# Queries of the first eight blocks through VectorE, and a later start for the second group's weights

## The chip, the cores and the metric

The kernel runs on one core of one Trainium2 chip. The metric is the device time of one launch in microseconds (us). Engines are named as the profile names them: PE is TensorE (matmuls), PEld its weight loads, DVE VectorE, ACT ScalarE, POOL GpSimd, and SP SyncE, the queue that issues nearly all DMAs, in program order.

## The reference

Two stages, one after the other, all in float32:

```python
# q, k, v: (8 batches, 8 heads, 576 tokens, 64)
scores = scale * q @ k.T
Dmat   = where(i >= j, gamma[h] ** (i - j), 0)     # a decay per head
x      = (scores * Dmat) @ v                       # -> (4608 tokens, 512)
h      = x @ w_in                                  # w_in (512, 2048)
out    = (h * erf(softplus(h))) @ w_out            # w_out (2048, 512)
```

The weights come as float64 and are rounded to float32 in the kernel.

## The kernel before

**Attention.** The 4608 tokens are cut into 36 blocks of 128 (`pieces`): of each batch's 576 tokens four blocks, and the last 64 tokens of two batches share one. So blocks 8, 17, 26 and 35 are two-piece blocks. The work on a block is three functions: `transposes(i)` makes qT and kT (64 of the head dimension x 2 heads on the partitions), `scores(i)` multiplies them on PE and lets DVE apply the decay mask (tile sT), `outputs(i)` multiplies sT by v, adds the running state of the batch, and lets DVE scale the result into x. The list `stages` puts `transposes(i + 1)` ahead of `outputs(i)` and `scores(i + 1)` behind it (L68 to L73); `attend(n)` works that list off. Four PSUM tiles with the tag "at" serve all three.

**Two ways to a transpose.** From block SQUARES = 8 on, q and k are loaded as squares (`load_squares`, L122): 32 partitions per DMA, four DMAs per one-piece block and name, 112 KB each, with a contiguous run of 896 bytes per row and head; a DVE transpose of 32 x 32 squares (L314) then gives qT or kT. For a two-piece block it is eight DMAs of 48 KB with runs of 384 bytes. In blocks 0 to 7 they come as rows (`load_rows`, L135): two DMAs of 128 KB per block and name, runs of 256 bytes, then four PE transposes into PSUM (L320) and an ACT copy (L322 for q, L326 for k). k of one-piece blocks and v are always loaded as rows too, for the outputs. The square tiles have two buffers per name (q's rows use the same two buffers), k's and v's row tiles four. `transposes(i)` ends by issuing the q load (and the k squares, if any) of block i + 2, `outputs(i)` that of k and v of block i + 3.

**Two big products.** Nine chunks of 512 tokens, and four groups of the 2048 hidden columns: 36 pairs (g, c), group by group. Each pair has a `First` (x times w_in, then softplus, erf, multiply) and a `Second` (times w_out, added to the running output). Both use seven products in place of eight for a 2 x 2 block product (Strassen-Winograd), so operands are sums of quarters, made by DVE (`tt`, L99). One product is 8 matmuls of 256 columns: L478 in `First`, L585 in `Second`. The first chunk of the first group uses the plain product (L532).

**Order of the work.** A string in the main part (L708) interleaves the first chunk by hand: `a` is one attention stage, `p` a part of the plain product, `w` loads one part of weights, a digit so many rounding steps. Then the loop L735 runs over `First(n + 1)` and `Second(n)` in turn, and `run(steps, rounds)` puts one attention stage and a given number of rounding steps behind every product. Nine chunks of group 0 carry all the attention, so it ends about a third of the way in (the last squares are turned at 318 us).

**Weights.** A group has eight parts of 512 KB (four of w_in, two DMAs each; four of w_out, one DMA each). `load_weights()` issues the next part into a ring of four buffers (`wraw`, L224). `rounding()` (L232) is a generator that rounds one part in five steps: an ACT pair (L246, L247), three DVE steps (L251, L255, L259), and a last step with DVE (L264) and POOL or DVE (L266, L267), which for groups 1 to 3 also issues the next part. The last part of w_in and of w_out is followed by four steps of sums (L99). The first eight parts are issued by the string; the loop issues two more at the head of the second and two at the head of the third block `First` (n = 1 and 2).

Of the kernel before, what the change touches and what calls it, by code (L numbers as in the profile page):

```python
# [11 lines left out]
FP32 = mybir.dt.float32  # L12
# [6 lines left out]
P = 128  # L19
B, H, S, D = 8, 8, 576, 64  # L20
D_MODEL, D_FF = 512, 2048
NP = H // 2
# [32 lines left out]
def kernel(  # L55
# [10 lines left out]
    nc = tc.nc  # L66
# [65 lines left out]
                )  # L132
        return t

    def load_rows(i, name, src, bufs):  # L135
        if name == "q":
            t = raw.tile([P, NP, P * D // SQ], FP32, tag="qs", name="raw_q", bufs=bufs)
            t = t.rearrange("p a x -> p (a x)")[:, : H * D].rearrange("p (h d) -> p h d", h=H)
        else:
            t = raw.tile([P, H, D], FP32, tag=name, name=f"raw_{name}", bufs=bufs)  # L140
        for b, s0, n, r0 in pieces[i]:
            for e in range(2):
                heads = src[b, e * NP : (e + 1) * NP, s0 : s0 + n, :]
                nc.sync.dma_start(out=t[r0 : r0 + n, e::2, :], in_=heads.rearrange("h p d -> p h d"))  # L144
        return t

    def load(i, names="qkv"):
        if i < len(pieces):
            t = loaded.setdefault(i, {})
            for name in names:  # L150
                src = {"q": q, "k": k, "v": v}[name]
                if name == "q" and i < SQUARES:
                    t["q"] = load_rows(i, "q", q, 2)
                elif name == "q":
                    t["qs"] = load_squares(i, "q", q)
                    t["ks"] = load_squares(i, "k", k)
                elif name == "v" or len(pieces[i]) == 1:
                    t[name] = load_rows(i, name, src, 4)

    load(0)  # L160
    cst = cpool.tile([P, CONST_COLS], FP32, name="cst")
# [13 lines left out]
    A11, S3, A12, A22, S1, S2, S4 = range(7)  # L175
    B11, T3, B21, B22, T1, T2, T4 = range(7)
    weights = {}

    def operands(name, g):
        if (name, g) not in weights:  # L180
# [51 lines left out]
    def rounding():  # L232


        while True:
            while not words or words[0][2] > most_g[0]:
                yield
            t, name, g, slot, j, sums = words.pop(0)
            w = operands(name, g)
            dst = w[:, slot : slot + 2, j, :]  # L240
            pairs = t[:, :].rearrange("p (h f two) -> p h f two", h=2, two=2)
            pairs_f = t[:, :].bitcast(FP32).rearrange("p (h f two) -> p h f two", h=2, two=2)
            low, high = pairs[:, :, :, 0], pairs[:, :, :, 1]
            r_f, high_f = pairs_f[:, :, :, 0], pairs_f[:, :, :, 1]
            a_f, a = dst, dst.bitcast(UINT32)
            nc.scalar.activation(a_f, high_f, AF.Abs)  # L246
            nc.scalar.mul(out=r_f, in_=low, mul=2.0**-52)  # L247
            yield


            nc.vector.tensor_scalar(  # L251
                out=a_f, in0=a_f, scalar1=HIGH_LEAST, scalar2=HIGH_MOST, op0=ALU.max, op1=ALU.min
            )
            yield
            nc.vector.tensor_scalar(  # L255
                out=a, in0=a, scalar1=3, scalar2=0x3FFFFFFF, op0=ALU.logical_shift_left, op1=ALU.bitwise_and
            )
            yield
            nc.vector.scalar_tensor_tensor(  # L259
                out=a, in0=high, scalar=0xC0000000, in1=a, op0=ALU.bitwise_and, op1=ALU.bitwise_or  # L260
            )
            yield

            nc.vector.tensor_scalar(out=high, in0=a, scalar1=0xFF800000, scalar2=None, op0=ALU.bitwise_and)  # L264
            engine = nc.vector if (name, g) == ("wa", 0) else nc.gpsimd
            engine.tensor_tensor(out=r_f, in0=high_f, in1=r_f, op=ALU.mult)  # L266
            engine.tensor_tensor(out=a_f, in0=a_f, in1=r_f, op=ALU.add)  # L267
            if g > 0:
                load_weights()
            yield  # L270
            if sums:
                yield from sums(*(w[:, i] for i in range(7)))

    round_step = rounding()

    def round_weights(n=1):
        for _ in range(n):
            next(round_step, None)
# [24 lines left out]
    def transposes(i):  # L303
        t = live[i] = loaded.pop(i)
        if i < SQUARES:
            weigh_values(i)
        for name in "qk":
            tT = t[name + "T"] = att.tile([P, NP, P], FP32, tag=name + "T", name=name + "T")
            if i >= SQUARES:
                for _, _, n, r0 in pieces[i]:  # L310
                    a = r0 // SQ * D
                    squares = t[name + "s"][:, :, a : a + n // SQ * D].rearrange("p h (a d) -> p h a d", d=D)
                    order = "p h (a r) -> p h a r" if name == "q" else "p h (r a) -> p h a r"
                    nc.vector.transpose(  # L314
                        out=tT[:, :, r0 : r0 + n].rearrange(order, r=SQ), in_=squares[:, :, :, :SQ]
                    )
            else:
                pt = ps_at.tile([P, NP, P], FP32, tag="at", name=f"pt_{name}")
                for p in range(NP):
                    nc.tensor.transpose(pt[:, p, :], flat(t[name][:, 2 * p : 2 * p + 2, :]), ident)  # L320
                if name == "q":
                    nc.scalar.copy(  # L322
                        out=tT.rearrange("p h (a r) -> p h a r", r=SQ), in_=pt.rearrange("p h (r a) -> p h a r", r=SQ)
                    )
                else:
                    nc.scalar.copy(out=tT, in_=pt)  # L326
        load(i + 2, "q")

    def scores(i):
# [139 lines left out]
    class First:  # L469
# [3 lines left out]
            self.g, self.c = g, c  # L473

        def product(self, a, acc, start):
            for j in range(GP):
                for d in range(2):
                    nc.tensor.matmul(  # L478
                        acc[:, j * TH : (j + 1) * TH],
                        lhsT=weights["wa", self.g][:, a, d, j * P : (j + 1) * P],  # L480
                        rhs=x[self.g, self.c][a][:, d, :],
                        start=(start and j == 0 and d == 0),
                        stop=(d == 1),
                        skip_group_check=True,
                    )
# [83 lines left out]
    class Second:  # L569
# [9 lines left out]
                nc.sync.dma_start(out=self.o, in_=od[self.c])  # L579

        def product(self, b, acc, start):
            left = self.of.left[b]
            for j in range(GP):
                for tp in range(2):
                    nc.tensor.matmul(  # L585
                        acc[:, tp, :],
                        lhsT=left[:, j * TH + tp * P : j * TH + (tp + 1) * P],
                        rhs=weights["wb", self.g][:, b, j, :],
                        start=(start and j == 0 and tp == 0),
                        stop=(j == GP - 1),  # L590
                        skip_group_check=True,
                    )
# [142 lines left out]
    for b, nxt in zip(blocks[1:], blocks[2:] + [None]):  # L735
        n = order.index((b.g, b.c))
        if isinstance(b, First):
            most_g[0] = order[n - 1][0] + 1
            if n in (1, 2):
                load_weights()  # L740
                load_weights()
            run(b.middle(), (1, 1))
            firsts[n - 1].sums()
            run(seconds[n - 1].first(), (1, 1) if n > 1 else ())
            run(b.last(), (1,) if 1 < n < n_ch else ())
            most[0] = before_chunk(n + 3)
        elif n + 2 < n_s:
            f = firsts[n + 1]
            for step, _ in enumerate(b.middle()):
                attend(min(done[0] + 1, most[0]))  # L750
                if step == 0:
                    f.erf()
                elif step == 1 and n + 2 >= n_ch:
                    operands_x(*order[n + 2])
            if n + 2 < n_ch:
                attend(after_chunk(n + 2))
                operands_x(*order[n + 2])
            run(nxt.first(), (1,))
            f.multiply()
            seconds[n + 1].begin()  # L760
            if n_ch <= n + 3 < n_s:
                load_x(*order[n + 3])
            run(b.last(), (0, 1))
        elif n + 1 < n_s:
            firsts[n + 1].erf()
            seconds[n + 1].begin()
            rest = b.rest()
            for _ in range(3):
                next(rest)
            firsts[n + 1].multiply()  # L770
            run(rest)
            firsts[n + 1].sums((0,))
            first = nxt.first()
            next(first)
            firsts[n + 1].sums((1,))
            run(first)
        else:
            run(b.rest())
# [30 lines left out]
```

## Time and profile before

| | us |
|---|---|
| median of 8 runs | 1039.12 |
| lowest, highest | 1037.62, 1040.63 |
| the profiled execution | 1038.71 |
| its span, first to last instruction | 1036.9 |
| busy: PE, PEld | 1017.8, 874.8 |
| busy: DVE, ACT, POOL | 675.9, 387.6, 125.1 |
| moved by DMA | 167.27 MB, mean 161 GB/s |

The profile's first part gives busy time per engine; PE's is an upper figure, since matmuls overlap and their ends are modelled. The second part cuts the span into 40 slices of some 26 us and writes the busy share of each in tenths. The fourth follows the chain of work that ended last back to the start. The other views are asked of the trace: busy time in chosen stretches, the instructions in order of time (start, length, engine, line, operation, tile written and tiles read, count, and in brackets the idle time before it and what ended it), groups of instructions with count, busy time and mean length, and who waited for whom.

### The profile page before, as it was taken

To read this page: it belongs to the slowest core of one execution; us is meant where nothing else is said; L and a number is where in the kernel's file an instruction comes from. 1 tells how busy PE (TensorE), PEld (TensorE's weight loads), DVE (VectorE), ACT (ScalarE), POOL (GpSimd) and SP (SyncE) were. 2 spreads that over 40 slices of the span, in tenths; PEclk is the share of its full clock that TensorE was granted. 3 is DMA by queue.
4 is the path that set the end of the run, shared out by engine and by line. 5 is a ranking of instruction groups with operands and counts; after the bars stand their busy time and mean duration, and the time that the engine had idled before them with its cause. 6 is when DMAs were issued, how large, how long until landed. Compare 5 with 4: busy or idle time off the path is not lost.

```text
span 1036.9 us, 15904 instructions
## 1 busy us (share of the span) xinstructions
PE 1017.8 (98%) x6322; PEld 874.8 (84%) x6322; DVE 675.9 (65%) x1063; ACT 387.6 (37%) x477; POOL 125.1 (12%) x122
## 2 busy tenths in 40 slices
PE   9899999999999999999999999999999999999998
PEld 8777877778788888888888888888888888888887
DVE  3998867778877645567665656666666655555555
ACT  2353233232342444433443334434443333333332
POOL 2161222321312100100001000100100000000000
PEclk9999999999999999999999999999999999999999
DMA  9989989979984531633274424353333334444433
GB/s 196 214 209 222 253 172 251 217 183 247 230 196 143 176 129 40 233 153 142 61 264 143 164 101 142 143 212 150 125 122 122 122 121 130 131 131 132 127 88 116
DMA packets 148778, 167.27 MB, mean 161 GB/s; under 512 B 97632, under 2 KB 123360, under 8 KB 140640
## 3 DMA queue, kind: packets, MB, share of 16 engines
q1 hardware_dynamic: 147696, 165.47, 56.2%
q8 instruction: 50, 0.82, 0.4%
q10 hardware_dynamic: 1008, 0.79, 0.3%
q14 instruction: 24, 0.20, 0.1%
HBM read 119.02 MB, written 47.19 MB: 160 GB/s over the span
## 4 chain that ended last, share of the span: by engine, by line
PE 79%; DMA 9%; DVE 5%; SPq 5%; issue 1%; ACT 1%; POOL 1%; DVEq 0%; POOLq 0%; ACTq 0%
PE a L585 21%; PE a L478 21%; PE g L585 11%; PE g L478 11%; PE e L585 5%; PE e L478 5%; SPq L130 3%; DMA raw_qs<-in_q_dram 2%; DMA raw_v<-in_v_dram 2%; DMA raw_ks<-in_k_dram 2%; PE s L335 2%; PE o L353 1%; SPq L144 1%; DVE x L99 1%; DVE t L99 1%
## 5 line engine op out<-in xcount | busy, mean ns | idle before, releaser
L478 PE MATMUL a<-x,wa 128*128 128x256 f32 x1120 | 267.6, 382 | 0.0
L478 PEld LDWEIGHTS a<-x,wa 128*128 128x128 f32 x1120 | 212.6, 191 | 30.0 <-issue 0.2
L585 PE MATMUL a<-wb,s 128*128 128x256 f32 x864 | 205.7, 381 | 0.0
L585 PEld LDWEIGHTS a<-wb,s 128*128 128x128 f32 x864 | 162.9, 190 | 23.6 <-ACT o L599 0.7
L99 DVE TENSOR_TENSOR t<-g,t 128x512 f32<-128x512 f32 x70 | 48.3, 690 | 151.5 <-ACT t L508 113.3
L478 PE MATMUL g<-x,wa 128*128 128x256 f32 x560 | 133.2, 381 | 0.5 <-DVE o L99 0.5
L478 PEld LDWEIGHTS g<-x,wa 128*128 128x128 f32 x560 | 105.7, 190 | 15.7 <-DVE o L99 0.9
L99 DVE TENSOR_TENSOR o<-a,o 128x512 f32<-128x512 f32 x108 | 74.2, 687 | 50.4 <-PE a L585 50.4
L503 ACT COPY t<-a 128x512 f32<-128x512 f32 x35 | 20.5, 586 | 188.4 <-PE a L478 188.4
L99 DVE TENSOR_TENSOR t<-t,s 128x1024 f32<-128x1024 f32 x72 | 87.6, 1258 | 0.0
L266 POOL TENSOR_TENSOR wraw<-wraw 128x512 f32<-128x512 f32 x28 | 29.4, 1050 | 463.8 <-DVE wraw L264 252.8
L547 ACT ACTIVATE s<-t 128x1024 f32<-128x1024 f32 x72 | 72.1, 1048 | 34.1 <-DVE t L99 34.1
L99 DVE TENSOR_TENSOR x<-x 128x512 f32<-128x512 f32 x116 | 77.9, 704 | 1.2
L514 ACT COPY t<-a 128x512 f32<-128x512 f32 x35 | 20.5, 586 | 153.0 <-PE a L478 153.0
L551 ACT ACTIVATE s<-s 128x1024 f32<-128x1024 f32 x72 | 72.1, 1049 | 0.4
L585 PE MATMUL g<-wb,s 128*128 128x256 f32 x288 | 68.6, 381 | 1.3 <-DVE t L99 1.3
L585 PE MATMUL a<-wb,t 128*128 128x256 f32 x288 | 68.6, 381 | 1.1 <-DVE t L99 1.1
L585 PE MATMUL e<-wb,t 128*128 128x256 f32 x288 | 68.6, 381 | 0.0
L585 PE MATMUL g<-wb,t 128*128 128x256 f32 x288 | 68.2, 380 | 0.0
L478 PE MATMUL e<-x,wa 128*128 128x256 f32 x280 | 66.8, 381 | 0.0
L99 DVE TENSOR_TENSOR o<-g,o 128x512 f32<-128x512 f32 x72 | 49.3, 685 | 25.6 <-ACT o L599 20.8
L585 PEld LDWEIGHTS g<-wb,s 128*128 128x128 f32 x288 | 54.3, 190 | 9.1 <-DVE t L99 1.6
(75 smaller groups left out, 1193.7 us busy)
## 6 DMA issues: line engine op xcount, KB each, us to landing
od<-o SPq DMA_DIRECT2D x54, 512.0 KB, 3.3
x<-xd SPq DMA_DIRECT2D x27, 1024.0 KB, 5.0
o<-od SPq DMA_DIRECT2D x27, 1024.0 KB, 4.9
raw_qs<-in_q_dram SPq DMA_DIRECT2D x96, 112.0 KB, 4.6
raw_ks<-in_k_dram SPq DMA_DIRECT2D x96, 112.0 KB, 4.2
xd<-x SPq DMA_DIRECT2D x9, 1024.0 KB, 5.3
raw_k<-in_k_dram SPq DMA_DIRECT2D x64, 128.0 KB, 4.5
raw_v<-in_v_dram SPq DMA_DIRECT2D x64, 128.0 KB, 4.7
```

The source lines that it names most:

```text
L99: nc.vector.tensor_tensor(out=out, in0=in0, in1=in1, op=op)
L130: nc.sync.dma_start(out=t[part * SQ : (part + 1) * SQ, :, at : at + m - SQ], in_=tokens[:, :, d0 : d0 + m - SQ])
L144: nc.sync.dma_start(out=t[r0 : r0 + n, e::2, :], in_=heads.rearrange("h p d -> p h d"))
L266: engine.tensor_tensor(out=r_f, in0=high_f, in1=r_f, op=ALU.mult)
L335: nc.tensor.matmul(ps[e][:, p, :], lhsT=t["kT"][heads[e], p, :], rhs=t["qT"][heads[e], p, :], start=True, stop=True)
L353: nc.tensor.matmul(o[p % 2][heads[(e + p) % 2], p // 2, :], lhsT=t["v"][:, 2 * p + e, :], rhs=t["sT"][:, e, p, :], start=(p < 2), stop=(no ...
L478: nc.tensor.matmul(acc[:, j * TH : (j + 1) * TH], lhsT=weights["wa", self.g][:, a, d, j * P : (j + 1) * P], rhs=x[self.g, self.c][a][:, d, :],
L503: nc.scalar.copy(out=self.t1[:, 1], in_=self.a)
L514: nc.scalar.copy(out=self.t2[:, 0], in_=self.a)
L547: nc.scalar.activation(self.s[:, j], t, AF.Softplus)
L551: nc.scalar.activation(self.s[:, j], self.s[:, j], AF.Erf)
L585: nc.tensor.matmul(acc[:, tp, :], lhsT=left[:, j * TH + tp * P : j * TH + (tp + 1) * P], rhs=weights["wb", self.g][:, b, j, :], start=(sta ...
```

## The change

Two things change together. First, `load` loads q of every block as squares, so that `transposes` turns q on DVE in blocks 0 to 7 as well; k keeps its rows and PE transposes there. Second, the weights of group 1 are asked for later and two parts ahead in place of four: one part at the end of `First` n = 2 and one at the end of n = 3 (before: two at the head of n = 1 and two at the head of n = 2). The rounding steps of the second and third block are left out except the two that end group 0's rounding (`First` n = 1), and three steps are added in `Second` n = 6, 7 and 8. A set `rounded` with two asserts is filled while the program is built; it issues no instruction.

```diff
-    def load_rows(i, name, src, bufs):
-        if name == "q":
-            t = raw.tile([P, NP, P * D // SQ], FP32, tag="qs", name="raw_q", bufs=bufs)
-            t = t.rearrange("p a x -> p (a x)")[:, : H * D].rearrange("p (h d) -> p h d", h=H)
-        else:
-            t = raw.tile([P, H, D], FP32, tag=name, name=f"raw_{name}", bufs=bufs)
+    def load_rows(i, name, src):
+        t = raw.tile([P, H, D], FP32, tag=name, name=f"raw_{name}")
...
-                if name == "q" and i < SQUARES:
-                    t["q"] = load_rows(i, "q", q, 2)
-                elif name == "q":
+                if name == "q":
                     t["qs"] = load_squares(i, "q", q)
-                    t["ks"] = load_squares(i, "k", k)
+                    if i >= SQUARES:
+                        t["ks"] = load_squares(i, "k", k)
                 elif name == "v" or len(pieces[i]) == 1:
-                    t[name] = load_rows(i, name, src, 4)
+                    t[name] = load_rows(i, name, src)
...
-            if i >= SQUARES:
+            if name + "s" in t:
...
-                pt = ps_at.tile([P, NP, P], FP32, tag="at", name=f"pt_{name}")
+                pt = ps_at.tile([P, NP, P], FP32, tag="at", name="pt")
                 for p in range(NP):
                     nc.tensor.transpose(pt[:, p, :], flat(t[name][:, 2 * p : 2 * p + 2, :]), ident)
-                if name == "q":
-                    nc.scalar.copy(
-                        out=tT.rearrange("p h (a r) -> p h a r", r=SQ), in_=pt.rearrange("p h (r a) -> p h a r", r=SQ)
-                    )
-                else:
-                    nc.scalar.copy(out=tT, in_=pt)
+                nc.scalar.copy(out=tT, in_=pt)
...
             most_g[0] = order[n - 1][0] + 1
-            if n in (1, 2):
+            run(b.middle(), (1, 1) if n != 2 else ())
+            firsts[n - 1].sums()
+            run(seconds[n - 1].first(), (1, 1) if n > 2 else ())
+            run(b.last(), (1,) if 2 < n < n_ch else ())
+            if n in (2, 3):
                 load_weights()
-                load_weights()
-            run(b.middle(), (1, 1))
-            firsts[n - 1].sums()
-            run(seconds[n - 1].first(), (1, 1) if n > 1 else ())
-            run(b.last(), (1,) if 1 < n < n_ch else ())
             most[0] = before_chunk(n + 3)
         elif n + 2 < n_s:
...
                     operands_x(*order[n + 2])
+                elif step == 2 and n_ch - 4 < n < n_ch:
+                    round_weights()
...
-            run(nxt.first(), (1,))
+            run(nxt.first(), (1,) if n > 1 else ())
             f.multiply()
...
-            run(b.last(), (0, 1))
+            run(b.last(), (0, 1) if n > 1 else ())
```

More of the change, by code (lines that the diff above doesn't have):

```diff
@@ L177 @@
     weights = {}
+    rounded = set()
     def operands(name, g):
@@ L271, in rounding @@
             if sums:
-                yield from sums(*(w[:, i] for i in range(7)))
+                for step, _ in enumerate(sums(*(w[:, i] for i in range(7)))):
+                    if step == 3:
+                        rounded.add((name, g))
+                    yield
     round_step = rounding()
@@ L475, in product @@
         def product(self, a, acc, start):
+            assert ("wa", self.g) in rounded
             for j in range(GP):
@@ L581, in product @@
         def product(self, b, acc, start):
+            assert ("wb", self.g) in rounded
             left = self.of.left[b]
```

## The prediction

> **What bounds it now.** I read the page first, then busy time by stretch, the chain of waits, the timeline where TensorE (PE) stands still, and the DMA issues.
>
> ```profile
> span 1036.9 us, 15904 instructions
> ...
> DMA  9989989979984531633274424353333334444433
> ...
> PE 79%; DMA 9%; DVE 5%; SPq 5%; issue 1%; ACT 1%; POOL 1%; DVEq 0%; POOLq 0%; ACTq 0%
> ```
>
> PE holds 79% of the chain; transfers, VectorE (DVE) and the SyncE queue (SPq) hold 19%, and DMA is saturated only in the first dozen slices, some 310 us. So the change can act only there. The stretches (engine columns are busy us):
>
> ```profile
> 38.00:63.00 25.00, 24.52 (x249) 19.79 (x248) 23.17 (x40) 12.24 (x22) 8.34 (x8) 1.00 0.89 206
> 63.00:84.00 21.00, 17.33 (x161) 13.69 (x160) 20.76 (x32) 7.48 (x9) 10.04 (x8) 1.00 1.01 262
> 84.00:340.00 256.00, 250.16 (x2309) 204.01 (x2309) 192.11 (x326) 82.91 (x108) 58.04 (x57) 0.99 0.90 207
> ```
>
> The third busy column is DVE: 23.2 of 25 us, then 20.8 of 21. From 38 to 84 us DVE sets the pace, from 84 on PE does. To size PE's slack I took, from the timeline, the time from the first matmul of one group of 8 (or 16) to the first of the next, less the same pair's usual time (8 matmuls of L478 or L585: 1.73 us, 1.92 before scores). The excess from 84 us to the end is only 9.2 us, and 7.0 of it lies in five places where keys or queries come late: 139.4 (0.83), 153 to 158 (1.36), 175.5 (0.44), and 187 to 191 (2.62, 0.20, 1.54). The last one in the timeline:
>
> ```profile
> 174.44 0.88 SPq L229 DMA_DIRECT2D wraw<-in_moe_w_out_dram  x1
> ...
> 182.96 0.71 DVE L314 STREAM_TRANSPOSE qT<-raw_qs 128x512 f32<-128x512 f32 x1 [3.67 <-DMA raw_qs<-in_q_dram]
> ...
> 185.77 1.09 DVE L314 STREAM_TRANSPOSE kT<-raw_ks 128x512 f32<-128x512 f32 x1 [2.10 <-DMA raw_ks<-in_k_dram]
> ...
> 187.00 1.37 PE L335 MATMUL s<-qT,kT 64*128 64x128 f32 x16 [2.54 <-DVE kT L314]
> ...
> 188.30 3.43 PE L478 MATMUL a<-x,wa 128*128 128x256 f32 x8
> ```
>
> Half a MB of weights stands in SP's queue just ahead of the squares that PE then waits for, and after the wait 8 matmuls take 3.43 us instead of 1.73: the clock record grants half speed from 187.8 to 191.2.
>
> **The change, part by part.**
>
> *Queries of blocks 0 to 7.* Out go, per block, four PE transposes and a ScalarE (ACT) copy; in comes one DVE transpose, whose row exists in later blocks:
>
> ```profile
> L320 PE MATMUL pt_q<-ident,raw_q 128*128 128x128 f32 x32 | 5.4, 295 | 2.0 <-DMA raw_q<-in_q_dram 2.0
> ...
> L322 ACT COPY qT<-pt_q 128x512 f32<-128x512 f32 x8 | 4.7, 586 | 21.9 <-PE pt_q L320 21.9
> ```
>
> ```profile
> L314 DVE STREAM_TRANSPOSE qT<-raw_qs 128x512 f32<-128x512 f32 x5 | 3.5, 702 | 0.9 <-DMA raw_qs<-in_q_dram 0.9
> ```
>
> PE's and ACT's saving (about 0.44 us of PE start to start and 0.59 of ACT per block) I cost at nothing: PE's start-up holds 42 idle matmuls, and its transposes stand where it waits for sT anyway. The most it could give back is the 2.2 us that pt_q waited for a PSUM tile held by sT.
>
> DVE pays 8 x 0.70. In blocks 0 to 4 it lies while PE does the outputs, DVE being busy 4.9 of the first 20 us: nothing. Block 5 is dearer, by order:
>
> ```profile
> 31.44 0.43 DVE L251 TENSOR_SCALAR wa<-wa 128x512 f32<-128x512 f32 x1 [0.48 <-ACT wa L246]
> ...
> 34.36 1.56 DVE L267 TENSOR_TENSOR wa<-wa,wraw 128x512 f32<-128x512 f32 x1
> ...
> 36.84 1.27 DVE L99 TENSOR_TENSOR sT<-s,cst 128x512 f32<-128x512 f32 x2
> ```
>
> The string of the first stage puts five rounding steps ahead of this block's transposes. Today qT comes from ACT at 32.4 and scores start at 34.76; DVE gets to it at 35.92 and ends at 36.6, scores (1.1 us) end at 37.75, sT starts at 37.8 instead of 36.84: **+1.0**. Blocks 6 and 7 fall in the full stretch: 2 x 0.70, of which the 0.83 us that DVE waits for ACT at 54.2 takes one: **+0.7** (0 to 1.4).
>
> SP issues four DMAs for two. A row issue takes 0.51, a square's 0.43, with 0.04 between: 4 x 0.47 - 2 x 0.53 = 0.82 us a block. Five queries lie ahead of the second weights part, whose landing starts the chain at 31.44: 4.1 us. Against it, three issues there (6.65, 14.15, 20.15) took 1.19, 1.66, 1.81 instead of 0.51, 3.1 us in which SP waited for nothing named; I read them as backlog of packets, and a query now makes 512 packets instead of 1024. So **+1.0**. The packet records bound it: 256 B take 18 ns undisturbed, 896 B 41, and 66 (median) under load in the later blocks; a query costs 1024 x 18 / 16 = 1.15 us of the 16 engines today, 1.31 or 2.11 then, +0.16 to +0.96 a block, 7.7 us for eight at worst. Sum of the start-up: **+2.7**, bounds -2.2 and +10.1 (7.7 + 1.0 + 1.4).
>
> The Trainium skill ("DMA: Bandwidth & Descriptors", Specifications) has 512 bytes as the least transfer for line rate. The packet times agree in direction (14 bytes a ns for 256 B, 22 for 896 B), but the change reads 448 KB for 256, so by the rows the gain is eaten; by the rule alone, halving the rate below 512 B as an estimate, the start-up would lose its +1.0.
>
> *From 63 to 84 us* DVE's work is unchanged, so the delay passes through.
>
> *Weights.* Today's issues: two parts (512 KB each) at 82.84, two at 123.94, one each at 146.02, 174.44, 205.76, 232.10, 283.65, 312.44. After: none for the first two blocks, one at the end of the third, one inside and one after the fourth, then one per finished part: by SP's lag of some 15 to 20 us behind PE about 150, 185 and 190, then 220, 250 and so on. Up to 180 us six parts become one.
>
> ```profile
> 123.94 2.72 SPq L229 DMA_DIRECT2D wraw<-in_moe_w_in_dram  x4
> ```
>
> ```profile
> DVE kT L314 <- DMA raw_ks<-in_k_dram: 13.6, 12, 2.1
> DVE qT L314 <- DMA raw_qs<-in_q_dram: 13.3, 8, 3.7
> ```
>
> The queue is in order and two square buffers deep: loads for block 16, issued right behind those four, land late (DVE waits 2.73 and 1.31 at 136 to 138). Without them SP gains 2.7 us, and 512 KB at the 230 GB/s of full stretches is 2.3 us a part. Block 21's squares, 2.5 us late at PE, come in time. Taken: 0.8 of the first place, 0.7 of the second (a two-piece block's 20 small issues stay), 0.4, and all 4.4 of the last, clock included: **-6.3** (bounds 0 and -8.6, with 1.6 us at 223 and 262 where DVE is late). What is late next: the two parts at 185 to 190 stand ahead of block 23's squares, which today make nobody wait; with SP 3 to 4 us further on I take **+0.7** (0 to 4.4, a second stall like the one at 187).
>
> *Rounding steps* move from 104 to 160 us into blocks 3 to 8, three of them new places; DVE is busy 15 to 16 of 20 us there: 0. Two parts in flight instead of four: a part is asked for five steps, 20 us, ahead; SP's longest wait for an output is 14.8 us and a landing 5.1, so ACT, which has the wait in its queue ahead of the next copies, barely waits: 0 (to +2).
>
> **Sum:** 2.7 - 6.3 + 0.7 = -2.9. The profiled execution took 1038.71 us (span 1036.9 and 1.8 around it), 0.4 under the median of 1039.12; on the median the forecast is **1036.2**.
>
> The skill's "TensorE: Matmul & The Clock Gate" (Part 1) says that an idle window of about 3.4 us halves PE's clock; here 2.5 us did it at 187 and 2.1 at 29.6 did not. It speaks against the change: without pt_q, PE idles from 29.6 to beyond 33. By the rule that is up to 1.7 us more, and the sum -1.2.
>
> **Rivals.**
> - *The start-up is free:* the stalls of SP vanish wholly and DVE's waits take the transposes: 0 - 5.6, **1033.5**. For it: SP's 6 us of long issues before 31 us. Against: DVE's 23.2 of 25.
> - *The stall only moves:* 1 MB at 185 to 190 makes block 23 late as at 187, with the half clock: +4.4 for +0.7, so +0.8, **1039.9**. Against: SP's head start.
> - *Slower: the start-up is set by transfers.* Squares at 66 ns a packet in the saturated first 50 us cost 7.7, DVE 1.7, less 5.6: +3.8, **1042.9**. It decides from a start-up loss of 7.7 us (5.6 + 2.1), that is from a mean packet of 59 ns. For it: 2048 and 256 B packets swell from 18 to 24 ns and more there. Against: only a third of the packets are queries.
> - *The weights were not to blame:* squares come late by the stores and the two buffers; relief 2.0, net +0.7, **1039.8**.
>
> **Chances.** 0.2% is 2.1 us, about what a measurement can tell from no change. Forecast 0.36 (own range 1034.5 to 1037.9; faster 0.30, same 0.06), free start-up 0.18 (faster), moved stall 0.16 (same), transfers 0.20 (slower), weights not to blame 0.10 (same 0.06, slower 0.04): faster 0.48, same 0.28, slower 0.24. The range 1032.5 to 1043 reaches from the free start-up to the transfers.
>
> **What would show it.** Start-up: the first matmul of L478 (62.77 today) at 65 to 66. Block 5: qT on DVE behind L267. Weights: no wait of scores for kT between 130 and 190, no half clock near 188, first weights of group two on SP near 150. Wrong it is if L478 starts after 70 (transfers) or before 63.5 (free), or if scores wait by more than 2 us between 195 and 215.

## The result and the profile after

The changed kernel takes 1044.28 us (median of 11 runs, 1041.29 to 1046.47) beside 1038.73 for the kernel before (32 runs): 1.0052 times as long, with a 95% interval of 1.0041 to 1.0062. The forecast was 1036.2; it went the other way, and the time lies beyond the upper end of the range. The profiled execution took 1045.99 us (span 1043.3), 1.7 above its median, so sums from the trace come out some 1.7 us too dear.

Lines move a little: L478 is now L473, L585 is L581, L335 is L329, L320 (PE's transposes) is L319, L314 is L313, L267 is L263.

The page's first line, its DMA row and the shares of the chain of waits, after:

```profile
span 1043.3 us, 15878 instructions
...
DMA  9989979979994444444445444444433334444423
...
PE 84%; DMA 7%; DVE 5%; SPq 2%; issue 1%; ACT 1%; POOL 0%; DVEq 0%; POOLq 0%; ACTq 0%
```

PE holds 84% of the chain instead of 79, and the kernel is slower: a share is an average, and says nothing about where time was lost. That is read from starts of the same work in both traces. In each column stands how many us later than before the changed kernel starts a batch of scores (one batch a block, counted from 0) or, in the last two, a big product (counted from the first one of the plain product):

| scores 1 | 3 | 4 | 5 | 8 to 15 | 16 | 18 | 20 | 22 | 25 | 31 | product 108 | 114 and all later |
|---|---|---|---|---|---|---|---|---|---|---|---|---|
| +4.96 | +4.67 | +8.41 | +9.59 | +8.84 | +8.01 | +6.65 | +6.21 | +1.96 | +1.39 | +2.66 | +2.66 | +5.90 |

Four terms: start-up (up to the first matmul of L478 or L473, which is as late as scores 8) **+8.84**, waits taken away **-7.45**, waits that come back later **+1.27**, and a new one at 349 to 358 us **+3.24**. From there to the end PE keeps its distance.

**Start-up.** Busy time from 0 to the first matmul of L478 or L473, before and then after (columns: length, PE, PEld, DVE, ACT, POOL, then granted clock, DMA share, GB/s):

```profile
0.00:62.77 62.77, 57.82 (x651) 48.49 (x651) 43.14 (x77) 23.10 (x38) 17.17 (x23) 1.00 0.94 196
```

```profile
0.00:71.61 71.61, 57.20 (x619) 47.70 (x619) 48.29 (x85) 19.64 (x31) 17.67 (x23) 0.93 1.01 195
```

PE is no busier, DVE has its 5.1 us more. The two right columns tell the story: the DMA engines were full or nearly so in both, at the same 195 to 196 GB/s, for 62.8 and then for 71.6 us. By the packet records 12.39 MB are moved up to that matmul before and 14.0 after; eight queries of 448 KB in place of 256 are 1.57 MB more. Scores 4, which start at 28.5 us before, already have 8.41 of the loss, so it arises ahead of the stretch from 38 us on. What PE waited for in that stretch, after:

```profile
PE pt L319 <- DMA raw_k<-in_k_dram: 7.2, 3, 3.5
PE s L329 <- DVE qT L313: 2.5, 1, 2.5
```

It is the keys, whose rows did not change, that come late; they share SP's queue and the DMA engines with the queries. And the forecast's block 5 (its transpose behind the rounding steps) is there, dearer than costed:

```profile
42.17 1.42 DVE L263 TENSOR_TENSOR wa<-wa,wraw 128x512 f32<-128x512 f32 x1
...
43.51 0.70 DVE L313 STREAM_TRANSPOSE qT<-raw_qs 128x512 f32<-128x512 f32 x1
...
44.36 1.16 PE L329 MATMUL s<-qT,kT 64*128 64x128 f32 x16 [2.47 <-DVE qT L313]
```

**Weights.** Between 125 and 195 us PE's list of waits is empty after, where before scores waited 4.1 us for kT there; no half clock is left near 188. The first parts of group 1 are asked for at these times:

```profile
151.42 2.65 SPq L225 DMA_DIRECT2D wraw<-in_moe_w_in_dram  x2
189.56 3.84 SPq L225 DMA_DIRECT2D wraw<-in_moe_w_in_dram  x4
```

**The hand-over at 349 us.** Here a `Second` hands over to a `First`, and PE's product of tile g needs a PSUM tile that DVE frees with `o<-g,o`. The timeline before, then after:

```profile
341.79 2.61 DVE L99 TENSOR_TENSOR x<-x 128x512 f32<-128x512 f32 x4
...
347.79 0.68 DVE L99 TENSOR_TENSOR o<-g,o 128x512 f32<-128x512 f32 x1
...
348.53 1.99 PE L478 MATMUL g<-x,wa 128*128 128x256 f32 x8 [0.48 <-DVE o L99]
...
348.96 1.35 POOL L266 TENSOR_TENSOR wraw<-wraw 128x512 f32<-128x512 f32 x1 [19.82 <-DVE wraw L264]
```

```profile
344.79 4.43 DVE L99 TENSOR_TENSOR x<-x 128x512 f32<-128x512 f32 x4
...
345.01 1.36 POOL L262 TENSOR_TENSOR wraw<-wraw 128x512 f32<-128x512 f32 x1 [16.41 <-ACT wb L242]
...
346.45 1.61 POOL L263 TENSOR_TENSOR wb<-wb,wraw 128x512 f32<-128x512 f32 x1
...
352.01 0.68 DVE L99 TENSOR_TENSOR o<-g,o 128x512 f32<-128x512 f32 x1
...
352.74 3.19 PE L473 MATMUL g<-x,wa 128*128 128x256 f32 x8 [2.03 <-DVE o L99]
```

Before, POOL's two rounding operations come after the sums of x. After, they run beside them, the same four sums take 4.43 us instead of 2.61, PE waits 2.03 instead of 0.48, and the eight matmuls that follow take 3.19 instead of 1.99, at half clock.

### The profile page after: what moved, and what is told of

The parts are those of the page before. It is cut to its first block, busy times and chain, and to the rows that moved or that the text cites. A ratio compares the mean times of both kernels' runs of the same rounds, so it can differ in the third digit from the quotient of the medians.

```text
span 1043.3 us, 15878 instructions
## 1 busy us (share of the span) xinstructions
PE 1016.9 (97%) x6290; PEld 874.0 (84%) x6290; DVE 683.0 (65%) x1071; ACT 383.8 (37%) x469; POOL 125.7 (12%) x122
## 4 chain that ended last, share of the span: by engine, by line
PE 84%; DMA 7%; DVE 5%; SPq 2%; issue 1%; ACT 1%; POOL 0%; DVEq 0%; POOLq 0%; ACTq 0%
PE a L581 22%; PE a L473 22%; PE g L473 11%; PE g L581 11%; PE e L581 6%; PE e L473 5%; PE s L329 2%; PE o L347 2%; DMA raw_qs<-in_q_dram 2%; DMA wraw<-in_moe_w_in_dram 1%; DVE x L99 1%; DMA wraw<-in_moe_w_out_dram 1%; PE o L370 1%; SPq L140 1%; DMA raw_v<-in_v_dram 1%
## 5 line engine op out<-in xcount | busy, mean ns | idle before, releaser
L473 PE MATMUL a<-x,wa 128*128 128x256 f32 x1120 | 266.7, 381 | 0.0
L473 PEld LDWEIGHTS a<-x,wa 128*128 128x128 f32 x1120 | 212.1, 190 | 29.8
L581 PE MATMUL a<-wb,s 128*128 128x256 f32 x864 | 205.7, 381 | 0.0
L581 PEld LDWEIGHTS a<-wb,s 128*128 128x128 f32 x864 | 162.9, 190 | 23.6 <-ACT o L595 0.7
L473 PE MATMUL g<-x,wa 128*128 128x256 f32 x560 | 134.4, 383 | 2.0 <-DVE o L99 2.0
L473 PEld LDWEIGHTS g<-x,wa 128*128 128x128 f32 x560 | 106.3, 191 | 17.5 <-DVE o L99 2.4
L498 ACT COPY t<-a 128x512 f32<-128x512 f32 x35 | 20.5, 586 | 190.3 <-PE a L473 190.3
L509 ACT COPY t<-a 128x512 f32<-128x512 f32 x35 | 20.5, 586 | 152.7 <-PE a L473 152.7
L581 PE MATMUL a<-wb,t 128*128 128x256 f32 x288 | 68.6, 381 | 0.3 <-DVE t L99 0.3
L581 PE MATMUL e<-wb,t 128*128 128x256 f32 x288 | 68.6, 381 | 0.0
L581 PE MATMUL g<-wb,s 128*128 128x256 f32 x288 | 68.6, 381 | 0.0
L581 PE MATMUL g<-wb,t 128*128 128x256 f32 x288 | 68.2, 380 | 0.0
L473 PE MATMUL e<-x,wa 128*128 128x256 f32 x280 | 66.8, 381 | 0.0
L503 ACT COPY t<-a 128x512 f32<-128x512 f32 x35 | 20.5, 585 | 113.8 <-PE a L473 113.8
```

Of the source, the lines that this page charges most:

```text
L473: nc.tensor.matmul(acc[:, j * TH : (j + 1) * TH], lhsT=weights["wa", self.g][:, a, d, j * P : (j + 1) * P], rhs=x[self.g, self.c][a][:, d, :],
L498: nc.scalar.copy(out=self.t1[:, 1], in_=self.a)
L503: nc.scalar.copy(out=self.t2[:, 1], in_=self.a)
L509: nc.scalar.copy(out=self.t2[:, 0], in_=self.a)
L581: nc.tensor.matmul(acc[:, tp, :], lhsT=left[:, j * TH + tp * P : j * TH + (tp + 1) * P], rhs=weights["wb", self.g][:, b, j, :], start=(sta ...
```

## The experiments

**The two halves apart.** The kernel before with the new `load` and `transposes` alone, and with the new weight schedule alone:

> The kernel before with all queries as squares, its weight schedule as before. Theory (the start-up is set by the transfers of the squares): the first matmul of L478, at 62.8 us before and 71.6 with both changes, comes at 71 to 72, and the late keys and queries between 139 and 191 us are there again, so the time is 8 to 9 us over the kernel before, some 1047. Rival (the later waits are a race between PE and the loads, which a late PE loses less of): start-up the same, waits of 7.0 us shrink by half, some 1044.

> The kernel before with the later weights alone, queries of blocks 0 to 7 as rows. Theory (weights relieve 7 us, and the rounding step added in the seventh block costs 3.2 us near 350 us): L478 starts at 62.8, no wait of scores for keys over 0.9 us between 130 and 230, a stall of some 2 us and a half-clock window at 345 to 355: 3 to 4 us under the kernel before, some 1035. Rival (the relief was the late PE's doing, not the weights'): within 1 us of the kernel before, 1038 to 1042 with the stall near 350.

Squares alone: 1046.62 us beside 1039.22, ratio 1.007 (1.0055 to 1.0086); start-up +10.97 at scores 8, +9.28 at the end. Weights alone: 1035.99, ratio 0.9964 (0.995 to 0.9978); -7.5 at scores 22 to 24, -4.2 at scores 31, and a hand-over wait of 2.0 us gives back another part. So the loss belongs to the squares, and the schedule is a gain that was smaller than it could be. The relief of 7.5 us is the schedule's own, for PE is not late in that kernel; in the squares alone a late PE loses 4.2 us of the waits up to scores 22 (+10.97 to +6.73), and 3.5 of them come back by scores 26.

**The hand-over: which step does it?** The weights alone, less the step that the change adds in `Second` n = 6:

```diff
-                elif step == 2 and n_ch - 4 < n < n_ch:
+                elif step == 2 and n_ch - 3 < n < n_ch:
```

> As the weights alone, without the rounding step added in the seventh block (Second n = 6). Theory (POOL's two rounding operations stand beside the four x sums of DVE there, which take 4.43 us in place of 2.61, and PE waits for a PSUM tile): the stall near 350 goes, 3 us under the run of the weights alone, some 1032. Rival (the stall comes from how far the rounding has got, not from that step): as the weights alone, some 1035.

1036.35 us, 0.997 (0.996 to 0.998): no gain. The theory that this step alone makes the wait is refuted. Its timeline shows why:

```profile
337.94 2.61 DVE L99 TENSOR_TENSOR x<-x 128x512 f32<-128x512 f32 x4
...
341.03 1.04 POOL L266 TENSOR_TENSOR wraw<-wraw 128x512 f32<-128x512 f32 x1 [18.95 <-issue]
...
341.41 3.97 DVE L99 TENSOR_TENSOR t<-t,s 128x1024 f32<-128x1024 f32 x2
...
342.15 2.15 POOL L267 TENSOR_TENSOR wb<-wb,wraw 128x512 f32<-128x512 f32 x1
```

The sums have their 2.61 us back, but POOL's two operations only moved one DVE instruction on, and now the multiply `t<-t,s` takes 3.97 us (2.35 before). The new theory: two POOL operations anywhere in the DVE work between sums and `o<-g,o` do it. To test it, the step after it goes too, in the weights alone and in the whole change:

```diff
-            run(nxt.first(), (1,) if n > 1 else ())
+            run(nxt.first(), (1,) if n > 1 and n != n_ch - 3 else ())
```

> The new weight schedule alone, without the extra rounding step at the seventh chunk (as in the weights less one step) and without the step in the first part that follows it, so that GpSimd has its steps there where the kernel before has them. Theory 'any two GpSimd operations beside VectorE between the sums of x and o make TensorE's hand-over late': no GpSimd operation lies between the sums and o, VectorE's sums take 2.6 instead of 4.4 us and its multiply 2.35, the wait of the next big product falls from 2.0 to 0.7 us, and the time is 1.0 to 1.8 us under 1036.35 (the weights less one step): 1034.5 to 1035.3. Theory 'the place does not matter, the steps left out here come due elsewhere': another wait appears at a later step and the time stays within 0.4 us of 1036.35.

> The changed kernel whole, with those two rounding steps left out at the seventh chunk. In the changed kernel the wait at 349 to 358 us (2.2 us, then 1.8 us of half clock) cost 3.24 us against the kernel before. Theory 'GpSimd beside VectorE': it goes, 1044.28 becomes 1040.5 to 1041.5, and what is left over the kernel before (1.5 to 2.5 us) is start-up less the weights' relief. Theory 'the phase of the whole chain': the wait stays and the time is within 0.7 us of 1044.28.

Weights alone: **1033.94 us**, 0.9937 (0.9922 to 0.9952), the lowest median here. Whole change: 1041.74, 1.0012 (0.9997 to 1.0027), 2.5 under the changed kernel. In the weights alone PE's list of waits is empty from 335 to 362 us, and the DVE work has its old lengths with POOL behind it:

```profile
338.99 2.61 DVE L99 TENSOR_TENSOR x<-x 128x512 f32<-128x512 f32 x4
...
342.13 2.35 DVE L99 TENSOR_TENSOR t<-t,s 128x1024 f32<-128x1024 f32 x2
...
344.39 0.69 DVE L99 TENSOR_TENSOR o<-g,o 128x512 f32<-128x512 f32 x1
...
345.55 1.04 POOL L266 TENSOR_TENSOR wraw<-wraw 128x512 f32<-128x512 f32 x1 [22.42 <-issue]
```

The theory held for the wait and the lengths; the time is 0.6 us under the range it gave. The whole change lands somewhat above what was expected (1041.74 for 1040.5 to 1041.5): its hand-over wait is gone too, but by its trace other waits have come in ahead of it (+0.71 at scores 25, +3.42 from scores 29 on).

**The start-up: issues or bytes?** Several kernels here are the same program up to the first product, so their profiles show how far one start-up scatters. With the queries as squares (the changed kernel, the squares alone, the changed kernel with two steps left out) that product comes at 71.61, 73.74 and 69.32 us; with rows (the kernel before and three versions of its weights) at 62.77, 62.78, 63.92 and 64.46. Differences of less than some 4 us between two single start-ups with squares, or 2 us between two with rows, say nothing. The means differ by 8.1 us.

First, queries by rows as before, but in four DMAs of 64 KB instead of two of 128: the issues of the squares without their bytes.

```diff
-                nc.sync.dma_start(out=t[r0 : r0 + n, e::2, :], in_=heads.rearrange("h p d -> p h d"))
+                for half in (range(0, NP, 2) if name == "q" else ()):
+                    nc.sync.dma_start(
+                        out=t[r0 : r0 + n, e + 2 * half : e + 2 * half + 3 : 2, :],
+                        in_=heads[half : half + 2].rearrange("h p d -> p h d"),
+                    )
+                if name != "q":
+                    nc.sync.dma_start(out=t[r0 : r0 + n, e::2, :], in_=heads.rearrange("h p d -> p h d"))
```

> The kernel before, each row load of q in blocks 0 to 7 cut into four DMAs of 64 KB in place of two of 128 KB: as many issues as squares, the old bytes and packets. Theory (transfers): L478 starts within 1.5 us of 62.8, time within 2 us of the kernel before. Rival (SP's issues set the start-up): L478 starts 5 us late or more, some 1044.

1044.47 us, 1.0047 (1.0031 to 1.0064); start-up **+4.04**, nearer to the rival, though short of its 5 us. Then the squares with half of the bytes:

```diff
+        few = NP // 2 if i < SQUARES else NP
...
-                    out=t[part * SQ : (part + 1) * SQ, :, at : at + m - SQ], in_=tokens[:, :, d0 : d0 + m - SQ]
+                    out=t[part * SQ : (part + 1) * SQ, :few, at : at + m - SQ], in_=tokens[:, :few, d0 : d0 + m - SQ]
...
```

> The squares alone, of which only the first two of four pairs of heads are loaded for blocks 0 to 7 (half the bytes and half the 896-byte packets, as many issues); VectorE transposes these two twice, so the other two pairs' scores are those of the wrong heads and the output differs from the reference. VectorE has one instruction more a block. Theory 'packets and bytes': k of block 1 lands 1 to 2 us earlier than in the squares alone, start-up loss 4 to 7 us instead of 11.0, time 1040 to 1043. Theory 'number of issues': loss stays over 9 us, time over 1045.

1040.90 us, 1.002 (1.0004 to 1.0036); start-up **+5.58** instead of 10.97, and scores 1 only +0.95. That lies in the bytes theory's band: half of the start-up's loss went with half of the bytes, and by medians 7.4 us over the kernel before became 1.7. But the bytes are now fewer than those of the rows (224 KB for 256), and 5.6 us are left in the profile; the four issues and VectorE's part remain to explain them. Last, the other side, bytes without issues: rows in two DMAs, the first of which reads eight heads in place of four (128 KB a block more).

```diff
+            wide = 2
...
-                heads = src[b, e * NP : (e + 1) * NP, s0 : s0 + n, :]
...
+                m = NP * wide if e == 0 else NP
+                heads = src[b, e * NP : e * NP + m, s0 : s0 + n, :]
...
```

> The kernel before, in which the first of the two row loads of each query of blocks 0 to 7 reads eight heads in place of four: 384 KB a block in place of 256, as many issues, 256-byte runs as before; the heads read too much lie in the tile unused. That is 1.05 MB more, where the squares bring 1.57 MB more. Theory 'the start-up moves its bytes at a fixed rate' (12.39 MB until the first product at 62.77 us in the kernel before, 14.0 MB until 71.61 in the changed one, both 196 GB/s): 1.05 MB / 196 GB/s = 5.3 us later (4 to 6.5), the first product at 67 to 69, time 1043 to 1045.5. Theory 'the number of issues alone': the first product within 1 us of 62.8, time within 1.5 us of the kernel before.

1044.38 us, 1.0054 (1.0031 to 1.0076); start-up **+4.60**, no more issues than before. The stretch up to the first product in the kernel with four issues, with half the squares, with more bytes, and in the squares alone:

```profile
0.00:66.81 66.81, 58.40 (x651) 48.55 (x651) 44.04 (x77) 23.61 (x39) 17.41 (x23) 0.97 0.83 180
```

```profile
0.00:68.35 68.35, 56.86 (x618) 46.94 (x619) 49.61 (x93) 19.25 (x31) 17.29 (x23) 0.95 0.82 182
```

```profile
0.00:67.37 67.37, 59.55 (x650) 49.27 (x650) 42.93 (x77) 23.12 (x38) 17.56 (x23) 0.97 0.98 196
```

```profile
0.00:73.74 73.74, 58.55 (x618) 49.08 (x618) 48.20 (x85) 19.24 (x31) 17.48 (x23) 0.88 0.96 196
```

The last two columns part the causes in the first three. With more issues the DMA engines fall to 0.82 or 0.83 busy and 180 GB/s; in the kernel with four issues SP issues almost without a gap up to 24 us, and seldom longer than usual, so it seems that SP can't feed them. With more bytes they stay at 0.98 and 196 GB/s: they are full. In the squares alone they are 0.96 busy at 196 GB/s, so by the same reading it is the bytes there: 1.57 MB at 196 GB/s are 8.0 us (an estimate), beside 8.1 between the means above.

How much the issues add to that is not shown. The profiles seem to say it: 1.05 MB cost 4.60, so 1.57 MB cost 6.9, and 6.9 + 4.04 = 10.9, the 10.97 of the squares alone. But that fit is luck. The 10.97 is the slowest of three start-ups, from the slowest of four executions, the 4.04 is from the fastest of four, and the medians do not add up:

| us over the kernel before | start-up of one profile | medians of the same round |
|---|---|---|
| squares alone | +10.97 | +7.4 |
| four issues, bytes as before | +4.04 | +5.3 |
| issues as before, 1.05 MB more | +4.60 | +3.7 |
| four issues, half the squares | +5.58 | +1.7 |

By medians the issues (5.3) and 1.57 MB (5.5) would make 10.8, where the squares cost 7.4. VectorE's own part, forecast at 1.7 us, is not told apart either.

**Issues taken off SP.** The squares alone, their loads on ACT's queue:

```diff
-                nc.sync.dma_start(
+                (nc.scalar if i < SQUARES else nc.sync).dma_start(
```

> The squares alone, with the loads of the squares of blocks 0 to 7 issued on ScalarE's queue; SP issues only keys, values and the rest. Bytes, packets, the order of VectorE's work stay. The squares alone cost 10.97 us at the eighth batch of scores. Theory 'issues on SP' (k of block 1 and the later k stand behind four issues a block): k0 to k5 land as in the kernel before or up to 1 us later, start-up loss falls from 11.0 to 2 to 5 us, time near 1040 to 1042, less what ScalarE's own issues (0.4 to 0.8 us each, in front of its evictions) cost. Theory 'packets' (896-byte packets share the DMA engines with those of k): k lands as late as before this edit, loss stays at 9 to 12 us, time 1045 to 1048.

1055.04 us, 1.0161 (1.013 to 1.0192); start-up +22.96, beyond both theories. ACT's own timeline:

```profile
0.73 9.66 ACTq L130 DMA_DIRECT2D raw_qs<-in_q_dram  x8
...
11.71 0.58 ACT L325 COPY kT<-pt_k 128x512 f32<-128x512 f32 x1
```

Eight issues hold ACT for 9.66 us (later groups of four for 3.12 to 8.16, where SP takes 1.8 to 2.9 for four in the squares alone), and the copy of kT stands behind them. It settles nothing about issues on SP; it shows that an issue is not free on a queue with work of its own.

**Block 5 ahead of the rounding steps**, in the squares alone:

```diff
-    for what in "alkakakawkakakawaa3awwa2aaa5aawwa5pap5ppwwca4pa5pa5paa5ps1":
+    for what in "alkakakawkakakawaa3awwa2aaaa5awwa5pap5ppwwca4pa5pa5paa5ps1":
```

> The squares alone, with VectorE's transposes of block 5 put ahead of the group of rounding steps in which they stand last. In the changed kernel the fifth batch of scores waits 2.47 us for them. Theory 'block 5 stands behind the rounding': that wait goes below 0.3 us and the first big product comes 1 to 2.5 us earlier than in the squares alone (73.7 to 71.2 to 72.7), the time 1044 to 1046. Theory 'the transfers are what is late': the squares of block 5 land only then, the wait stays within 0.5 us and so does the time, 1046.6.

1045.61 us, 1.0057 (1.0035 to 1.0079); first product at 71.82, in the first theory's band, but also in the spread of 69.32 to 73.74, so the gain of 1.9 us can't be told from no gain. The wait of scores for qT falls from 3.2 us in the squares alone to 0.8 (the theory had below 0.3), and the timeline shows that the order is not all of it: the transpose now stands ready and waits for its data.

```profile
37.72 0.71 DVE L313 STREAM_TRANSPOSE qT<-raw_qs 128x512 f32<-128x512 f32 x1 [1.56 <-DMA raw_qs<-in_q_dram]
...
38.67 1.09 PE L319 MATMUL pt_k<-ident,raw_k 128*128 128x128 f32 x4 [3.81 <-DMA raw_k<-in_k_dram]
```

Both cures together, half the squares and block 5 ahead:

> The squares alone, half of them loaded (two of four pairs of heads, transposed twice, so that half of the scores are those of the wrong heads) and VectorE's transposes of block 5 ahead of the rounding steps: two cures together, which alone brought the loss of the start-up from 10.97 us to 5.58 and to 9.05. Theory 'two separate causes': the loss is 5.58 - 1.92 = 3.7 us (3.0 to 4.3) at the eighth batch of scores. Theory 'one cause, VectorE's transposes late by the late squares': with half the squares block 5 is no longer late and the loss stays at 5.2 to 5.8.

One time, 1041.92 us; the loss is 4.2 us, nearer to two causes (3.7) than to one. It stays a weak answer: the three start-ups with whole squares lost 6.56, 8.84 and 10.97, so profiles differ from execution to execution by more than twice what the order of block 5 seemed to be worth (1.9).

**The half clock.** The squares alone, with 20 idle matmuls after the first scores and 14 at two later places:

> The squares alone, with 20 more idle matmuls after the first batch of scores and 14 more after the fourth batch and at the place where the fifth waits, so that TensorE is not idle there. In the squares alone three stretches of 3.4 to 6.8 us at half clock follow its waits (11.3 to 18.1, 31.8 to 38.6, 45.4 to 48.9). Theory 'half clock is a cost of its own': the half-clock stretches shrink by half or more and the first big product comes 2 to 5 us earlier than 73.7, time 1042 to 1045. Theory 'TensorE waits for data either way, and the half clock lies in the shadow of it': the clock is full and the time within 1 us of 1046.6, or later by the idle matmuls' own 1 to 3 us where data come earlier than they end.

1044.80 us, 1.0061 (1.0041 to 1.0081), start-up +9.35:

```profile
0.00:72.11 72.11, 65.46 (x714) 56.41 (x714) 48.59 (x85) 19.62 (x31) 17.27 (x23) 1.00 0.97 199
```

The clock is full all through (0.88 in the squares alone), and all but 1.6 us of the loss stays, short of the 2 to 5 us of the first theory and within the spread just named. The time, 1044.80, lies in the first theory's band and 0.8 us under the second's, so neither holds as put. What can be said: the first product comes at 72.11 with a full clock, and came at 69.32 with the clock at 0.93, so no price of the half clock shows beside the spread.

**Only blocks 6 and 7 as squares**, on top of the best schedule:

```diff
+    Q_SQUARES = SQUARES - 2
...
-                if name == "q" and i < SQUARES:
+                if name == "q" and i < Q_SQUARES:
```

> The new weight schedule with its steps in place, and squares through VectorE for blocks 6 and 7 alone (0 to 5 by rows as in the kernel before). TensorE saves two groups of four transposes, 0.9 to 1.1 us each, ScalarE two evictions, VectorE has two transposes more. Theory 'the loss is made by the first six blocks, whose data are late': the first big product comes 0 to 2 us earlier than 62.8 and the time is 0 to 2 us under the same kernel with rows. Theory 'VectorE is the bound of blocks 6 and 7': it comes 0.5 to 1.5 us later, time as much over.

1035.09 us, 0.9943 (0.9924 to 0.9963), not told apart from 1033.94; first product at 64.72 for 64.46. Squares in the last two blocks neither cost nor bring anything that shows, though at 196 GB/s their 0.39 MB more would be 2.0 us (an estimate); whether they are hidden by the spread of 1.7 us or by nothing waiting for them is open.

## Why the prediction was wrong

- **The failed step is the start-up, +2.7 for +8.84** (8.1 between the means of several profiles), and in it the +1.0 for SP and packets. The prediction took 4.1 us of extra issues ahead of the second weights part and set 3.1 us of long issues off against them, as a backlog of packets that fewer packets would end. It did not end: issues of over 0.7 us ahead of that part take 2.9 us too long in the changed kernel (3.1 before), and the part is issued 5.3 us later, not 1.0. Its issue before, then after:

```profile
22.56 1.21 SPq L229 DMA_DIRECT2D wraw<-in_moe_w_in_dram  x2
```

```profile
27.84 2.86 SPq L225 DMA_DIRECT2D wraw<-in_moe_w_in_dram  x2
```

With four issues and the old bytes it is issued at 26.27 (+3.7, and the long issues shrink to 1.2 us); with the old issues and more bytes at 25.22 (+2.7, and they grow to 5.8). So with rows the long issues shrink and grow with how busy the DMA engines are (0.83, 0.94 and 0.98), and half as many packets a query did not end them: the squares bring more bytes to engines that were 0.94 busy. The price of the bytes stood in the prediction as the bound of 7.7 us, and in the slower rival (loss above 7.7 us, 1042.9, chance 0.20). That rival comes nearest to what happened; what it lacks is the hand-over. Its packet time of 66 ns was measured at 73 (mean of the changed start-up), and the 256-byte packets beside them went from 22 to 27.

- **VectorE as the limit from 38 to 84 us:** from 38 to 63 us the prediction's own row has PE busier (24.52 of 25 us) than DVE (23.17), and 8.41 us of the loss were there by scores 4, at 28.5 us before.
- **The rule beside it.** The Trainium skill ("DMA: Bandwidth & Descriptors", Specifications) gives 512 bytes as the least transfer for line rate. Queries in packets of 896 bytes instead of 256 did not raise the rate of the whole here: 196 GB/s before, 195 after, 196 with more 256-byte packets.
- **Block 5, +1.0:** the place was right and the wait was 2.47 us. By the timelines two things meet there, the rounding and late data; their shares are not told apart.
- **PE's and ACT's saving at nothing:** not contradicted; apart from the first scores (7.44 for 7.84) nothing in the start-up came earlier.
- **The half clock at 30 us** came (granted half from 32.5 to 35.9), and another, not forecast, from 12.0 to 18.9; neither has a price of its own that the runs could show.
- **Weights, -6.3: right, also place by place** but for the second, which gave twice as much. Forecast 0.8, 0.7, 0.4 and 4.4; measured 0.83, 1.36, 0.44 and 4.25 (from +8.84 to +1.96 in the table).
- **Two new parts at 185 to 190, +0.7:** issued at 189.56; no wait between 195 and 215. Waits come at 245 and 285 instead (0.8 and 0.9 us), net of the old ones there +1.27; that the two parts cause them is not shown.
- **Rounding moves, 0:** wrong, +3.24. DVE had been checked for busy time and POOL not at all. What moved was the phase of POOL's two operations against DVE's chain to the hand-over. The Trainium skill ("SBUF — State Buffer", SBUF: two separate sides) says that a DVE instruction with two inputs in SBUF and a GpSimd instruction that reads SBUF lock each other out, and that the one that starts first holds the lock for its whole length. The traces agree: DVE's four sums gain 1.82 us beside two POOL operations that take 1.36 and 1.61, and in the other run the multiply gains 1.62. In the changed kernel the sum that starts just ahead of POOL (344.79) keeps its 0.69 us, and POOL's operation takes 1.36 where it takes 1.04 alone; and after 84 us the nine `t<-g,t` beside POOL's rounding, which have one input in PSUM, take 0.69 us as they do alone. No run was made to test the lock itself; that the loss goes with the overlap, the version with the steps in place shows.
- **Sum.** By medians the squares cost 7.4 us (alone), 8.3 (on the new schedule) and 7.8 (on the best one), the schedule brings 3.2, and 5.8 with its steps in place. The three figures for the squares lie around the 8.0 us of their bytes. The best kernel is the one without the squares.

## What to carry to other kernels

Where the DMA engines are full, count bytes first: a form of load that is easier for an engine but moves more bytes delays everything behind it, also tensors that did not change. Where the queue that issues can't keep them full, count issues too; here the busy share of the DMA engines told which of the two it was. Before adding up parts of a start-up from single profiles, see how far two profiles of the same program differ; here it was up to 4.4 us. When work on GpSimd moves, look at what VectorE does beside it at its new place, not only at how busy VectorE is.

## What was not expected of the hardware

- DVE's work stretches beside POOL's: four sums 2.61 to 4.43 us, a multiply 2.35 to 3.97.
- Issues of squares on ACT's queue took 0.8 to 2.0 us each, where SP's took 0.45 to 0.75 in the squares alone (both from groups of four or eight).
- With the DMA engines 0.94 busy or more, the rate of a start-up was 194 to 201 GB/s, whatever the mix of 256- and 896-byte packets.
- One program's start-up came 4.4 us apart in three executions (first product at 69.32, 71.61 and 73.74 us).
